# A pre-LN linear-attention block with an FFN on one core: the written order of 542 operations drawn anew, with the last five tiles' outputs finished in another sequence and the attention state copied on ScalarE

## The chip, the cores and the metric

The kernel runs on one core of a Trainium2 chip. The metric is device microseconds of that core, the median of three runs. The engines are named as in the profile: PE is TensorE's matmul, PEld its weight load, DVE is VectorE, ACT is ScalarE, POOL is GpSimd, and SP is the engine whose queue issues every DMA of this kernel.

## The reference

Inputs are bf16: x is 1 x 2048 x 512, wqkv 512 x 1536, wo 512 x 512, w1 512 x 1792, w2 1792 x 512. There are 32 heads of 16.

```python
phi = lambda t: jnp.where(t > 0, t + 1, jnp.exp(t)) + 1e-6
...
pq, pk = phi(q), phi(k)
kv = jnp.einsum("bhsd,bhse->bhde", pk, v)
z = jnp.einsum("bhsd->bhd", pk)
num = jnp.einsum("bhqd,bhde->bhqe", pq, kv)
den = jnp.einsum("bhqd,bhd->bhq", pq, z)[..., None] + 1e-6
o = num / den
...
x = A_x
h = x + _A_ref(_layernorm(x, axis=-1), A_wqkv, A_wo)
h2 = h + _B_ref(_layernorm(h, axis=-1), B_w1, B_w2)
return h2
```

`_A_ref` projects q, k and v, applies the attention above and the output projection wo; `_B_ref` is relu(x w1) w2.

## The kernel before, in words

The 2048 rows are 16 tiles t of 128 rows, in four chunks c of four tiles. Everything stays in SBUF, and PSUM is one tile `bk` of eight banks of 128 x 512 fp32. The body defines one small function `op_*` for each step. The string `ORDER` at the top lists 542 words, and the loop in lines 548 to 550 calls the functions in that order. A word is a name and its numbers: `K.5.3` is the key projection of tile 5 into bank 3, `f.13.4.7.7` is tile 13's second FFN product into bank 4, blocks 7 to 13. The order of the words on each engine is the order of that engine's queue; the framework adds the semaphore waits. No planner runs. What is moved in the string is moved on every engine that the word uses, SP's queue of DMA issues among them.

The steps, with the words that matter below:

- Layer norm of x: `lx` loads tiles; `S` and `A` are the statistics (DVE), `R` the two ACT steps of 1/sqrt, `N` the normalised tile (DVE). It is transposed either by PE (`T`) with a copy on ACT (`E`), for tiles 0 to 4, or by a DMA (`X`), for the others. `warm` is a run of matmuls on zeros into the bank that it names.
- Keys: `K` (four matmuls of 512 columns), then `F`, `U` on ACT and `M`, `D` on DVE for phi. `lk`, `lq`, `lv`, `lo`, `l1`, `l2` load rows of the weights. `G` accumulates phi(k)^T x-normalised in banks 4 to 7 over all tiles.
- Attention state: `gA` (ACT) or `gD` (DVE) copies two banks of that sum to `gT`; `kv`, `kx`, `m` make from it, wv and wo one 512 x 512 matrix per head block. `za`, `zf`, `z` sum the keys.
- Queries: `Q`, with `qF`, `qU`, `qM`, `qD` for phi. `dn`, `dnl`, `dnx` form 1/den, `dt` transposes it by DMA, `dm` scales the queries.
- `h` is the attention output of a tile (four matmuls), `hD` (DVE) adds x. `s`, `a`, `r`, `n` are the second layer norm; `x` transposes tile t by DMA to the chunk's `lnT`, `t` and `e` do it by PE and ACT for tile 2.
- FFN: `p.c.f.b` makes one block of 128 hidden columns for a whole chunk, so the first `p` of a chunk needs all four tiles' transposes. `pA` (ACT) or `pD` (DVE) is relu over two blocks. `f` is the product with w2: 14 matmuls for a tile, written as halves of seven; tile 15 is written as three column pieces of 128, 256 and 128.
- Output: `fo` (DVE) scales, adds h and writes to one of four buffers of `gT`; `fd` stores it (SP).

Of the kernel before, what the change touches and what calls it, by code (L numbers as in the profile page):

```python
# [23 lines left out]
lq.2.2 S.10 G.3 G.2 X.8 U.6.2 F.6.2 N.13 D.4.2 M.6.2 A.10 X.9 K.8.2 X.12 D.6.2 S.15 S.11 K.9.3 F.8.2 A.15 A.11
A.14 R.10.2 G.5 K.12.0 X.13 R.14.2 M.8.2 N.11 G.4 G.6 X.11 G.7 N.10 W.8.2 K.13.1 masks N.14 N.15 za.2 X.10 G.8
K.11.3 K.10.2 F.12.2 za.4 U.12.2 Q.0.0.0 F.10.2 X.14 U.10.2 Q.0.1.1 M.12.2 za.6 qU.0.0.2 G.9 M.10.2 X.15 K.14.2
l2.7.3 D.12.2 D.10.2 qF.0.0.2 G.12 K.15.3 za.8 qM.0.0.2 Q.0.2.0 za.10 F.14.2 lv.0.2 Q.0.3.1 U.14.2 za.12 M.14.2
D.14.2 G.13 G.10 zf.12 l1.2.2 G.11 G.14 qF.0.2.2 qM.0.2.2 G.15 z.0.2.14 z.3.2.14 z.2.2.14 lo.0.2 l2.0.3 z.1.2.14
Q.1.0.3 qD.0.0.2 qW.0.2.2 zc zh gA.0.2 dn.0.0 lv.2.2 Q.1.1.4 gD.2.2 l2.10.4 lo.2.2 kv.3.6 dnl.0 dnx.0.0.2
qF.1.0.2 kv.2.6 kv.0.6 dnx.0.2.2 kv.1.6 kx Q.1.2.0 Q.1.3.1 m.1.6 rt.2.2 m.0.5 qM.1.0.2 qW.1.0.2 rv.2 qF.1.2.2  # L30
dt.0 qM.1.2.2 dt.3 mA.0.2 Q.2.3.7 Q.3.1.3 dt.1 qW.1.2.2 m.3.5 l1.0.2 dm.0.0.2 m.2.4 Q.3.0.2 l2.3.4 mA.2.2 dn.1.1
dm.0.2.2 Q.2.2.6 h.3.5 h.0.0 h.2.4 hD.3 dnl.1 s.3 dnx.1.0.2 dnx.1.2.2 h.1.1 rt.6.5 hD.0 Q.3.2.0 qF.2.2.2
qU.3.0.2 a.3 dt.5 s.0 qF.3.0.2 hD.1 qU.2.2.2 a.0 hD.2 dt.4 n.0 Q.3.3.1 n.3 re.6 qF.3.2.2 Q.2.0.3 dt.7 s.1
qU.3.2.2 Q.2.1.4 dm.1.0.2 dm.1.2.2 a.1 h.4.6 qF.2.0.2 qM.2.2.2 x.0 n.1 qU.2.0.2 s.2 a.2 x.3 n.2 h.6.7 x.1 h.7.0
hD.6 t.2.5 s.6 h.5.1 qM.2.0.2 e.2 qD.2.2.2 qD.2.0.2 p.0.10.2 p.0.5.7 hD.5 dn.2.5 p.0.2.4 hD.4 dnl.2 hD.7
qM.3.0.2 p.0.11.3 dnx.2.0.2 qM.3.2.2 s.4 qD.3.2.2 s.5 a.6 r.0.4 dt.8 p.0.4.6 p.0.13.1 pA.0.10.2 dnx.2.2.2
p.0.0.2 dt.9 dt.11 p.0.1.3 p.0.12.0 pD.0.4.2 qD.3.0.2 pD.0.0.2 p.0.3.5 dt.10 dm.2.0.2 dn.3.2 dm.2.2.2 a.4
pA.0.12.2 dnl.3 dnx.3.0.2 n.6 p.0.6.6 p.0.9.3 h.8.0 p.0.7.7 pA.0.2.2 dnx.3.2.2 h.10.4 hD.10 hD.8 dt.12 x.6 s.7
dt.15 pA.0.6.2 p.0.8.2 dt.14 h.9.6 hD.9 s.10 h.11.0 pA.0.8.2 hD.11 f.3.2.0.7 a.7 a.5 dt.13 dm.3.0.2 f.0.4.0.7
f.2.7.0.7 n.5 n.4 dm.3.2.2 h.12.3 h.15.1 a.10 f.3.2.7.7 hD.12 hD.15 fo.3 h.14.0 s.9 a.9 n.10 n.7 f.2.7.7.7  # L40
f.0.4.7.7 f.1.1.0.7 s.15 s.11 fo.2 s.8 h.13.2 n.9 a.15 s.12 f.1.1.7.7 a.8 hD.14 x.5 n.8 x.7 s.14 a.11 a.12 x.4
hD.13 fd.3 p.1.10.0 s.13 p.1.3.6 a.13 fo.1 p.1.9.7 fo.0 n.15 p.1.7.2 p.1.6.1 n.12 fd.0 x.10 pA.1.6.2 p.1.12.3
n.13 a.14 p.1.2.5 p.1.13.4 pD.1.2.2 pA.1.12.2 fd.1 p.1.11.1 pA.1.10.2 x.8 n.11 x.11 p.1.5.5 r.12.4 p.1.4.4 n.14
# [5 lines left out]
f.8.5.7.7 p.3.11.2 p.3.1.7 fo.10 fo.8 p.3.12.3 pD.3.0.2 fo.11 fd.11 p.3.13.4 pA.3.12.2 pA.3.10.2 f.14.6.0.7
f.9.0.0.7 p.3.8.2 f.9.0.7.7 p.3.9.3 pA.3.8.2 fo.9 fd.8 f.12.5.0.7 f.12.5.7.7 f.14.6.7.7 fd.10 f.13.4.0.7 fd.9  # L50
# [530 lines left out]
```

## Time and profile before

| what | value |
|---|---|
| median of three runs | 171.25 us (171.04, 172.23, 171.25) |
| the profiled execution's own time | 170.93 us |
| its span, first to last instruction | 169.2 us |
| mean granted TensorE clock | 0.998 |
| PE, DVE, ACT busy | 162.3, 102.4, 65.5 us |
| moved by DMA | 15.36 MB, of it 7.86 read from and 2.10 written to HBM |

The lines of the timeline give start and length in us, then engine, line of the kernel, operation, tiles (output <- inputs) and how many in a row; a bracket names how long the engine stood idle before and what ended that. SPq is SP's DMA queue; its length is that of the issue, and the time to landing stands in a row of its own. Of the 875 matmuls, 859 have a record in this trace.

### The profile page before, as it was taken

The page shows a single profiled execution, that of the slowest core. Times are in us where ns is not written, and L with a number is a line of the kernel's source. Part 1 is how long each engine was busy: PE and PEld are TensorE (multiplying, and loading weights), DVE is VectorE, ACT ScalarE, POOL GpSimd, SP SyncE. Part 2 cuts the span into 40 slices and gives each one's busy share as a digit, 9 for nine tenths or more (in the row PEclk, how much of TensorE's full clock was granted, in tenths as well). Part 3 has the DMA queues.
Part 4 walks back from the last instruction along what each step waited for, and adds up shares of the span by engine and source line. Part 5 has one row for each costly group of instructions (what it writes and reads, how often), then busy time and mean ns, then how long its engine had stood idle before and what let it go on. Part 6 is the DMA issues. An engine that isn't in the chain of part 4 may idle for free.

```text
span 169.2 us, 2285 instructions
## 1 busy us (share of the span) xinstructions
PE 162.3 (96%) x859; PEld 76.2 (45%) x875; DVE 102.4 (61%) x202; ACT 65.5 (39%) x95; POOL 4.8 (3%) x21
## 2 busy tenths in 40 slices
...
DMA packets 29947, 15.36 MB, mean 91 GB/s; under 512 B 22640, under 2 KB 28784, under 8 KB 29936
## 3 DMA queue, kind: packets, MB, share of 16 engines
...
q8 instruction: 7, 0.11, 0.3%
q14 instruction: 4, 0.03, 0.1%
HBM read 7.86 MB, written 2.10 MB: 59 GB/s over the span
## 4 chain that ended last, share of the span: by engine, by line
PE 89%; DVE 5%; DMA 3%; issue 1%; ACT 0%
PE bk L510 29%; PE bk L530 28%; PE bk L307 8%; PE bk L494 8%; PE bk L351 8%; PE bk L299 6%; DVE st L226 3%; DMA x_nat<-in_A_x_dram 2%; DMA lnT<-h_nat 2%; PE bk L448 1%; DVE h_nat L251 1%; PE bk L392 1%; PE bk L404 1%; PE bk L270 0%; DVE mv L227 0%
## 5 line engine op out<-in xcount | busy, mean ns | idle before, releaser
L510 PE MATMUL bk<-lnT,w_sb 128*128 128x512 bf16 x219 | 51.0, 379 | 0.4
L530 PE MATMUL bk<-w_sb,at 128*128 128x512 bf16 (+2 forms) x249 | 50.9, 355 | 0.1
L516 ACT ACTIVATE at<-bk 128x1024 bf16<-128x1024 f32 x16 | 16.1, 1020 | 70.1 <-PE bk L510 70.1
L530 PEld LDWEIGHTS <-at 128*128 128x128 bf16 x252 | 23.6, 98 | 25.2
L538 DVE SCALAR_TENSOR_TENSOR gT<-bk,rstd,h_nat 128x512 bf16<-128x512 f32 (+2 forms) x18 | 12.0, 686 | 36.0 <-PE bk L530 28.8
L510 PEld LDWEIGHTS <-w_sb 128*128 128x128 bf16 x224 | 21.8, 98 | 26.0 <-issue 0.2
L521 DVE TENSOR_SCALAR at<-bk 128x1024 bf16<-128x1024 f32 x12 | 14.5, 1219 | 13.5 <-PE bk L510 13.4
L317 ACT ACTIVATE eb<-bk 128x1024 bf16<-128x1024 f32 (+1 forms) x17 | 16.6, 975 | 6.9 <-PE bk L299 6.7
L299 PE MATMUL bk<-wk_sb,lnT 128*128 128x512 bf16 x63 | 16.0, 380 | 1.4 <-DMA wk_sb<-in_A_wqkv_dram 1.0
L307 PE MATMUL bk<-lnT,wq_sb 128*128 128x512 bf16 x61 | 14.9, 379 | 0.2
L494 PE MATMUL bk<-m_sb,pqs 128*128 128x512 bf16 x61 | 15.0, 379 | 0.1
L351 PE MATMUL bk<-at,h_nat 128*128 128x512 bf16 x55 | 13.2, 379 | 0.1
L500 DVE TENSOR_TENSOR h_nat<-bk,x_nat 128x512 bf16<-128x512 f32 x16 | 10.6, 678 | 4.0 <-PE bk L510 2.2
L320 ACT ACTIVATE rb<-bk 128x1024 bf16<-128x1024 f32 (+1 forms) x13 | 12.4, 964 | 0.0
L226 DVE BATCH_NORM_STATS2 st<-x_nat 128x6 f32<-128x512 bf16 x16 | 10.5, 679 | 2.3 <-DMA x_nat<-in_A_x_dram 2.3
L228 DVE BATCH_NORM_STATS2 st<-h_nat 128x6 f32<-128x512 bf16 x16 | 10.9, 686 | 0.1
L299 PEld LDWEIGHTS <-lnT 128*128 128x128 bf16 x64 | 5.7, 98 | 9.3 <-ACT lnT L280 2.6
L351 PEld LDWEIGHTS <-h_nat 128*128 128x128 bf16 x64 | 6.3, 98 | 7.5
L494 PEld LDWEIGHTS <-pqs 128*128 128x128 bf16 x64 | 6.1, 98 | 7.5 <-DVE pqs L484 1.0
L307 PEld LDWEIGHTS <-wq_sb 128*128 128x128 bf16 x64 | 5.9, 97 | 6.3
L461 ACT ACTIVATE wk_sb<-ld 128x1024 bf16<-128x1024 f32 x8 | 8.3, 1050 | 0.1
L484 DVE TENSOR_TENSOR pqs<-pqT,rd 128x1024 bf16<-128x1024 bf16 x8 | 5.2, 685 | 3.8 <-DMA rd<-wk_sb 2.3
...
## 6 DMA issues: line engine op xcount, KB each, us to landing
...
w_sb<-in_B_w_dram SPq DMA_DIRECT2D x2, 384.0 KB, 5.7
...
```

Source lines behind the costliest of these rows:

```text
L226: op_S = lambda t: nc.vector.bn_stats(out=st[:, t, :], in_=x_nat[:, t, :])
L299: nc.tensor.matmul(bk[:, b, :], lhsT=lnT[c][:, kd, j * P : (j + 1) * P], rhs=wk_sb[:, kd, :], start=(kd == 0), stop=(kd == KD - 1),)
L307: nc.tensor.matmul(bk[:, b, :], lhsT=wq_sb[:, kd, j * P : (j + 1) * P], rhs=lnT[c][:, kd, :], start=(kd == 0), stop=(kd == KD - 1),)
L317: nc.scalar.activation(out=buf(eb, kind, i, n), in_=bank(at_bank[kind, i], n), func=ACT.Exp)
L320: nc.scalar.activation(out=buf(rb, kind, i, n), in_=bank(at_bank[kind, i], n), func=ACT.Relu)
L351: nc.tensor.matmul(bk[:, KD + kd, :], lhsT=ln_nat[:, t, kd * P : (kd + 1) * P], rhs=pk(t)[:, 0, :], start=(t == 0), stop=(t == NT - 1),)
L494: nc.tensor.matmul(bk[:, b, :], lhsT=pqs[:, (c * KD + jb) % NQ, j * P : (j + 1) * P], rhs=m_sb[:, jb, :], start=(jb == 0), stop=(jb == KD ...
L510: nc.tensor.matmul(bk[:, b, cols], lhsT=w1_sb[:, kd, f * P : (f + 1) * P], rhs=lnT[c][:, kd, cols], start=(kd == 0), stop=(kd == KD - 1),)
L516: nc.scalar.activation(out=acts[c % 2][:, f : f + n, :], in_=bank(at_bank["p", c, f], n), func=ACT.Relu)
L521: nc.vector.tensor_scalar(out=acts[c % 2][:, f : f + n, :], in0=bank(at_bank["p", c, f], n), scalar1=0.0, scalar2=None, op0=ALU.max,)
L530: nc.tensor.matmul(bk[:, b, 0 : w * P], lhsT=acts[c % 2][:, f, j * P : (j + 1) * P], rhs=w2_sb[:, f, k * P : (k + w) * P], start=(f == 0), ...
L538: nc.vector.scalar_tensor_tensor(out=o_t[:, t % NO, cols], in0=bk[:, at_bank["f", t, k], 0 : w * P], scalar=rstd2[:, t : t + 1], in1=h_nat ...
```

## The change

Only the string `ORDER` is changed. It has 542 words before and after. Other than the sequence, these words differ: some banks; `gD.2.2` becomes `gA.2.2`, so both copies of the attention state are on ACT; of the relus, five go from ACT to DVE (`pA.0.2`, `pA.3.4`, `pA.3.6`, `pA.3.8`, `pA.3.10` become `pD`) and two from DVE to ACT (`pD.2.0` and `pD.3.0` become `pA`); 11 warm-up matmuls stay 11, but before they are all ahead of `T.0`, and now nine are ahead of it and two behind it. The start and the end of the string:

```diff
-const lx.0.1 lx.1.1 lx.2.2 S.0 warm.1.1 table A.0 S.1 warm.1.1 R.0.1 N.0 A.1 lk.0.2 S.3 warm.9.1 S.2 T.0.5 R.1.1
+const lx.0.1 lx.1.1 S.0 lx.2.2 table A.0 S.1 R.0.1 A.1 R.1.1 lk.0.2 N.0 S.3 warm.9.6 S.2 T.0.1 warm.1.6 lk.2.2
...
-f.13.4.7.7 f.15.0.0.14.3.1 fo.13 fo.15.3.1 fo.14 fd.15.3.1 f.15.2.0.14.0.2 fo.12 fd.13 fd.14 fo.15.0.2
-f.15.4.0.14.2.1 fo.15.2.1 fd.12 fd.15.0.2 fd.15.2.1
+f.14.6.0.7 p.3.8.2 f.9.1.0.7 f.9.1.7.7 pD.3.8.2 fo.9 f.14.6.7.7 fd.8 f.15.0.0.14.3.1 fd.11 fd.9 f.13.7.7.7
+fo.15.3.1 fo.14 f.12.5.7.7 fo.13 fd.15.3.1 f.15.2.0.14.0.2 fo.12 fd.14 fd.13 fo.15.0.2 fd.12 f.15.6.0.14.2.1
+fo.15.2.1 fd.15.0.2 fd.15.2.1
```

First place, ACT's queue in the head, from the key projection of tile 0 on. L280 is the copy behind a PE transpose (`E`), L317 and L320 are `F` and `U`, L232 and L233 the two steps of `R`:

```order
 L317 ACTIVATE eb<-bk 128x512
 L320 ACTIVATE rb<-bk 128x512
-L280 ACTIVATE lnT_81<-bk 128x4x128 x2
+L280 ACTIVATE lnT_81<-bk 128x4x128
+L317 ACTIVATE eb<-bk 128x512
+L280 ACTIVATE lnT_81<-bk 128x4x128
 L232 ACTIVATE rstd<-mv,eps_73 128x2
 L233 ACTIVATE rstd<-rstd 128x2
 L320 ACTIVATE rb<-bk 128x512
-L317 ACTIVATE eb<-bk 128x512
```

Tile 1's `F` moves from behind the root of tiles 4 and 5 to a place ahead of it, between `E.3` and `E.2`, which change places with each other. On DVE, `A.1` moves from behind `N.0` to a place ahead of it:

```order
 L226 BN_STATS st<-x_nat 128x6
+L227 BN_AGGR mv<-st 128x2
 L251 TENSOR_SCALAR h_nat<-x_nat,mv,rstd 128x512
-L227 BN_AGGR mv<-st 128x2
 L226 BN_STATS st<-x_nat 128x6 x2
```

The first row is `S.1`, the third `N.0`, the last `S.3` and `S.2`; only the aggregate is moved.

Second place, SP's queue in the middle. L480 is `dt`, L292 is `x` (lnT_82 is chunk 1, lnT_83 chunk 2), L204 loads three blocks of w2 (`l2.0.3`), L545 is a store of the output:

```order
-L480 DMA_TRANSPOSE rd<-wk_sb 128x4x128 x5
+L480 DMA_TRANSPOSE rd<-wk_sb 128x4x128 x4
+L204 DMA w_sb<-in_B_w_dram 128x3x512
+L480 DMA_TRANSPOSE rd<-wk_sb 128x4x128 x2
 L292 DMA_TRANSPOSE lnT_82<-hn 128x4x128
-L480 DMA_TRANSPOSE rd<-wk_sb 128x4x128 x3
-L292 DMA_TRANSPOSE lnT_82<-hn 128x4x128 x3
-L545 DMA out_dram<-gT 128x512 x2
+L480 DMA_TRANSPOSE rd<-wk_sb 128x4x128 x2
+L292 DMA_TRANSPOSE lnT_82<-hn 128x4x128
+L545 DMA out_dram<-gT 128x512
+L292 DMA_TRANSPOSE lnT_82<-hn 128x4x128 x2
```

The load of w2's first three blocks, which stood among the other weight loads near 31 us, now stands behind the transposes of chunk 2's denominators, and the store of tile 3 (`fd.3`) now stands between `x.5` and the last two transposes of chunk 1, `x.7` and `x.4`. The words that lead from there to chunk 1's first `p`, after:

```text
h.15.4 hD.12 hD.15 fo.3 a.10 s.11 a.11 f.0.7.7.7 h.14.4 s.15 f.2.2.7.7 h.13.6 f.1.1.7.7 fo.2 a.15 n.10 a.9 hD.14 n.9
s.12 hD.13 a.8 x.5 fd.3 x.7 fo.0 x.4 fo.1 x.9 p.1.10.0
```

In the same way `lq.0.2` leaves the first loads, where `lv.2.2` now stands, for a place between `X.12` and `X.13`.

Third place, the last outputs on DVE (L538 is `fo`), with the semaphores that each waits for. Before:

```order
L538 SCALAR_TENSOR_TENSOR gT<-bk,rstd_103,h_nat 128x512 [waits DVE_49,DMAHW0_49,PE_49,Activation_49]
L538 SCALAR_TENSOR_TENSOR gT<-bk,rstd_103,h_nat 128x128 [waits DMAHW5_49,PE_49]
L538 SCALAR_TENSOR_TENSOR gT<-bk,rstd_103,h_nat 128x512 [waits DMAHW7_49]
L538 SCALAR_TENSOR_TENSOR gT<-bk,rstd_103,h_nat 128x512 [waits DMAHW6_49]
L538 SCALAR_TENSOR_TENSOR gT<-bk,rstd_103,h_nat 128x256 [waits PE_49,Activation_49]
L538 SCALAR_TENSOR_TENSOR gT<-bk,rstd_103,h_nat 128x128 [waits PE_49]
```

These are tile 13, the first piece of tile 15, tiles 14 and 12, and the two last pieces of tile 15: tiles 14 and 12 wait for no matmul of their own. After:

```order
L538 SCALAR_TENSOR_TENSOR gT<-bk,rstd_103,h_nat 128x128 [waits DMAHW7_49,DVE_49,PE_49]
L538 SCALAR_TENSOR_TENSOR gT<-bk,rstd_103,h_nat 128x512 [waits DMAHW5_49]
L538 SCALAR_TENSOR_TENSOR gT<-bk,rstd_103,h_nat 128x512 [waits DMAHW0_49,DVE_49,PE_49]
L538 SCALAR_TENSOR_TENSOR gT<-bk,rstd_103,h_nat 128x512 [waits DMAHW6_49,PE_49]
L538 SCALAR_TENSOR_TENSOR gT<-bk,rstd_103,h_nat 128x256 [waits PE_49]
L538 SCALAR_TENSOR_TENSOR gT<-bk,rstd_103,h_nat 128x128 [waits PE_49]
```

Now the first piece of tile 15 and tile 14 come first, and tiles 13 and 12 each wait for their own last matmuls. In SP's queue the stores follow as 15's first piece, 14, 13, 12 and 15's last two.

More of the change, by code (lines that the diff above doesn't have):

```diff
@@ L24 @@
[L24 to L43, printed above, removed]
@@ L49 @@
[L49 to L52 removed]
+const lx.0.1 lx.1.1 S.0 lx.2.2 table A.0 S.1 R.0.1 A.1 R.1.1 lk.0.2 N.0 S.3 warm.9.6 S.2 T.0.1 warm.1.6 lk.2.2
+A.3 lx.4.2 A.2 lx.6.2 warm.1.6 E.0 N.1 K.0.1.0.2 lx.8.4 T.1.4 R.2.2 K.0.1.2.2 N.3 N.2 S.5 E.1 S.4 T.3.5 T.2.7
@@ new lines @@
+G.8 K.11.3 K.10.2 F.12.2 za.4 za.6 M.12.2 U.12.2 F.10.2 Q.0.1.1 Q.0.0.0 G.9 D.12.2 M.10.2 U.10.2 qF.0.0.2 za.8
+D.10.2 G.12 X.15 X.14 lv.0.2 za.10 l2.7.3 l1.2.2 qU.0.0.2 lo.0.2 K.14.2 K.15.3 Q.0.3.1 G.10 qM.0.0.2 lo.2.2
+Q.0.2.0 G.13 za.12 qD.0.0.2 F.14.2 U.14.2 qF.0.2.2 M.14.2 D.14.2 zf.12 G.14 G.11 qM.0.2.2 z.2.2.14 G.15 z.1.2.14
+z.0.2.14 z.3.2.14 Q.1.0.3 qW.0.2.2 zc zh gA.0.2 dn.0.0 Q.1.1.4 gA.2.2 kv.1.5 dnl.0 dnx.0.0.2 qF.1.0.2 kv.2.5
+kv.0.5 kv.3.5 kx dnx.0.2.2 l2.10.4 Q.1.3.1 Q.1.2.0 m.1.6 rt.2.2 m.0.5 qM.1.0.2 qW.1.0.2 rv.2 Q.2.3.7 qF.1.2.2
@@ new lines @@
+dt.0 qM.1.2.2 mA.0.2 Q.3.1.3 dt.3 m.3.5 dt.1 m.2.4 qW.1.2.2 l2.3.4 l1.0.2 dm.0.0.2 Q.3.0.2 mA.2.2 dn.1.0
+dm.0.2.2 Q.2.2.6 h.3.5 dnl.1 hD.3 h.0.0 h.2.4 dnx.1.0.2 dnx.1.2.2 qF.3.0.2 s.3 qF.2.2.2 h.1.1 qU.2.2.2 rt.6.5
+hD.0 Q.3.2.0 a.3 dt.5 dt.4 s.0 qU.3.0.2 hD.1 a.0 hD.2 dt.7 n.0 Q.3.3.1 s.1 n.3 Q.2.1.4 re.6 qU.3.2.2 qF.3.2.2
+Q.2.0.3 dm.1.0.2 dm.1.2.2 qF.2.0.2 a.1 x.0 n.1 qU.2.0.2 s.2 qM.2.2.2 a.2 x.3 h.6.2 qM.2.0.2 n.2 x.1 h.7.0 h.4.6
+hD.6 t.2.5 hD.7 h.5.1 e.2 qD.2.2.2 qD.2.0.2 p.0.10.2 p.0.5.7 dn.2.5 hD.4 p.0.4.6 dnl.2 p.0.11.3 hD.5 s.4
```

28 lines of the change are left out of this document (19 added, 9 removed).

## The prediction

> **What bounds the kernel now.** I read the page first, then busy time in stretches, then the chain of waits in order of time, then the store queue at the end.
>
> ```profile
> span 169.2 us, 2285 instructions
> PE 162.3 (96%) x859; PEld 76.2 (45%) x875; DVE 102.4 (61%) x202; ACT 65.5 (39%) x95; POOL 4.8 (3%) x21
> ...
> 5.46:19.68 14.22, 12.64 (x69) 5.22 (x69) 13.88 (x41) 12.76 (x27) 0.67 (x3) 1.00 0.72 210
> 19.68:93.38 73.70, 73.25 (x426) 35.25 (x434) 61.87 (x121) 38.77 (x49) 0.00 (x0) 1.00 0.47 115
> 93.38:165.75 72.37, 72.00 (x357) 34.27 (x362) 24.02 (x33) 12.21 (x17) 0.00 (x0) 1.00 0.14 36
> 165.75:169.20 3.45, 0.22 (x4) 0.05 (x1) 0.38 (x2) 0.00 (x0) 0.00 (x0) 0.91 0.46 140
> ```
>
> In the stretches the first number is the length, then busy us of PE, PEld, DVE, ACT and POOL. From 19.68 to 165.75 PE is busy 145.25 of 146.07 us. The 0.82 us that are missing are 16 matmuls without a record (859 against 875 weight loads), each a false gap of 0.05 in the chain. So nothing waits there: with the same matmuls, a new order can gain nothing in those 146 us and can only open holes. Room exists in two places. In the head, 5.46 to 19.68, PE idles 1.58 us, but there DVE is busy 13.88 of 14.22: the head is DVE's stream. The other is the end.
>
> ```profile
> 108.06 6.04 PE bk L530 x28
> ...
> 154.50 0.75 DVE L538 SCALAR_TENSOR_TENSOR gT<-bk,rstd,h_nat 128x512 bf16<-128x512 f32 x1 [5.24 <-PE bk L530]
> 155.28 0.33 SPq L545 DMA_DIRECT2D out_dram<-gT  x1
> ...
> 165.79 1.39 SPq L545 DMA_DIRECT2D out_dram<-gT  x3
> 166.01 0.35 DVE L538 SCALAR_TENSOR_TENSOR gT<-bk,rstd,h_nat 128x128 bf16<-128x128 f32 x1 [0.23 <-PE bk L530]
> 166.78 0.40 SPq L545 DMA_DIRECT2D out_dram<-gT  x1
> ```
>
> The first row gives the price of a 512-wide matmul in a full stream: 6.04/28 = 0.216 us. The rest is the end: the last DVE operation is done at 166.36, and a store can be issued 0.03 us after DVE is done (155.25, 155.28), so at 166.39. It is issued at 166.78, because three stores stand in SP's queue, (1.39-0.40)/2 = 0.495 us apart. The end loses 0.39 us to that queue.
>
> **The change, part by part.**
>
> *The end.* Before, DVE took tiles 13, 14 and 12 one right behind the other once tile 13 was complete, and their stores piled up. Now tiles 14, 13 and 12 are completed in this order, 13 and 12 by seven matmuls each, 7 x 0.216 = 1.51 us apart. Count back from the last DVE operation, which starts at 166.01. The last group (14 matmuls of 128 columns) takes 14 x 0.054 = 0.76, the one before (14 of 256) 1.51. So tile 12 reaches DVE near 163.7, is done 0.75 later, near 164.5, and is stored then, not at 165.79. The 256 columns reach DVE at 165.25 and take between the 0.35 of 128 columns and the 0.75 of 512, say 0.5: their store goes out near 165.8 and frees SP near 166.3, before 166.39. The last store then waits for DVE alone: **-0.39**. Bounds: -0.39, and 0 if one store more still stands ahead. The output has four buffers, and the stores that must land before tiles 13, 12 and 15 may be written are issued some 3 us earlier; cover enough.
>
> *The head.*
>
> ```profile
> 4.31 0.66 DVE L226 BATCH_NORM_STATS2 st<-x_nat 128x6 f32<-128x512 bf16 x1
> 4.99 0.41 DVE L251 TENSOR_SCALAR h_nat<-x_nat,mv,rstd 128x512 bf16<-128x512 bf16 x1
> 6.84 0.59 PE L299 MATMUL bk<-wk_sb,lnT 128*128 128x512 bf16 x2 [0.98 <-DMA wk_sb<-in_A_wqkv_dram]
> 9.14 1.11 ACT L280 ACTIVATE lnT<-bk 128x512 bf16<-128x512 bf16 x2
> 10.43 0.29 ACT L232 ACTIVATE rstd<-mv,eps 128x2 f32<-128x2 f32 x1 [0.18 <-DVE mv L227]
> 11.29 0.40 DVE L251 TENSOR_SCALAR h_nat<-x_nat,mv,rstd 128x512 bf16<-128x512 bf16 x1
> 11.72 3.90 SPq L291 DMA_TRANSPOSE lnT<-h_nat  x3
> 19.67 0.33 PEld L299 LDWEIGHTS <-lnT 128*128 128x128 bf16 x3 [0.49 <-DMA lnT<-h_nat]
> ```
>
> The last hole of PE, at 19.67, waits for X.8, which stands behind X.5 to X.7 in SP's queue, and that queue starts at 11.72, when N.5 (11.29 to 11.69) is done. So N.5 sets the head. A.1 now goes ahead of N.0: it must wait for S.1's end at 4.97, and N.0 slips from 4.99 to about 5.1. That delay ends in PE's wait for wk_sb at 6.84, and the same work stands ahead of S.3, so DVE's stream moves by some 0.03. On ACT, E.3, F.1 and E.2 now come ahead of the square root for N.5. E.2 and E.3 took 1.11 us together from 9.14; a third of that kind, 0.5 more, puts the root's first step near 10.8 instead of 10.43 and the end of its second near 11.3 (each 0.2 to 0.3), so N.5 starts near 11.34. Sum of the head: **+0.05**. Bounds: -0.1 (DVE's stream holds no more) and +0.3 (if ACT's three slip further). lv.2.2 in the old place of lq.0.2 is a load of the same size. lq.0.2 is now issued behind X.12, takes 0.6 us of SP ahead of X.13, and is wanted only at the first Q, near 29.
>
> *The warm-up.*
>
> ```profile
> 1.25 4.27 PE L215 MATMUL bk<-m_sb 128*128 128x512 bf16 x11 [1.25 <-DVE ones L177]
> ...
> L215 PE MATMUL bk<-m_sb x11: 379/634/634, 1.2 to 5.1; 128*128 128x512 bf16 x11
> ```
>
> Eleven either way, but two of them now follow T.0, in the wait for wk_sb: two at 0.216 from about 5.8 are over by 6.84. Take 8 slow ones and 3 fast ones: (4.27 - 0.38 - 2 x 0.216)/8 = 0.43 us for a slow one, so the slow ones (634 ns long) end near 4.7 in both orders, and the clock comes up within the ninth: **0**. The Trainium skill, "TensorE: Matmul & The Clock Gate", Part 1: The HAM clock gate, speaks against opening a hole here: the array runs at half rate until about 3.4 us of sustained work have passed in a window that runs freely. This trace agrees on the length (1.25 to about 4.7), and by the page the sum stays 0 here unless the window's phase falls on the new hole.
>
> *The attention state, and relus that change engine.*
>
> ```profile
> L384 ACT ACTIVATE gT<-bk 128x1024 bf16<-128x1024 f32 x1 | 1.0, 1023 | 2.8 <-PE bk L351 2.8
> ...
> L387 DVE CAST gT<-bk 128x1024 bf16<-128x1024 f32 x1 | 1.2, 1217 | 0.0
> ...
> L516 ACT ACTIVATE at<-bk 128x1024 bf16<-128x1024 f32 x16 | 16.1, 1020 | 70.1 <-PE bk L510 70.1
> L521 DVE TENSOR_SCALAR at<-bk 128x1024 bf16<-128x1024 f32 x12 | 14.5, 1219 | 13.5 <-PE bk L510 13.4
> ```
>
> The second copy moves from DVE (1.22) to ACT (1.02), behind the first. PE did not wait for either, since query projections stood ahead of kv: **0** in each direction. Of the relus, net three go from ACT to DVE, 0.2 us longer each, 0.6 in all. The tightest is the last, tiles 8 and 9 of the last chunk: 14 matmuls (3.0 us) now stand between p.3.8 and the first reader, against some 1.5 us of DVE and latency: **0**. If that cover went, at most 0.6.
>
> *Two transfers moved behind other waits.* These decide the sign.
>
> ```profile
> 19.08 2.53 SPq L291 DMA_TRANSPOSE lnT<-h_nat  x2
> ...
> 25.73 1.03 PE L299 MATMUL bk<-wk_sb,lnT 128*128 128x512 bf16 x4
> 68.95 1.26 SPq L480 DMA_TRANSPOSE rd<-wk_sb  x1
> 77.68 4.70 PE L530 MATMUL bk<-w_sb,at 128*128 128x512 bf16 x21
> w_sb<-in_B_w_dram SPq DMA_DIRECT2D x2, 384.0 KB, 5.7
> ```
>
> l2.0.3, 384 KB, was loaded near 31 and is now issued behind the four transposes that end at 70.21. The first f wants it at 77.68. Two loads of that size took a median of 5.7 us: landed near 76, **0**. It would have to take over 7.4.
>
> ```profile
> 87.75 1.19 SPq L292 DMA_TRANSPOSE lnT<-hn  x1
> 89.37 1.35 SPq L292 DMA_TRANSPOSE lnT<-hn  x1
> 90.78 0.56 SPq L545 DMA_DIRECT2D out_dram<-gT  x1
> 93.22 2.75 PE L510 MATMUL bk<-lnT,w_sb 128*128 128x512 bf16 x12
> 94.19 1.38 DVE L538 SCALAR_TENSOR_TENSOR gT<-bk,rstd,h_nat 128x512 bf16<-128x512 f32 x2
> 95.59 0.36 SPq L545 DMA_DIRECT2D out_dram<-gT  x1
> 96.04 1.19 SPq L292 DMA_TRANSPOSE lnT<-hn  x1
> ...
> DMA to landing us min/median/max: 2.4/2.4/4.1
> ...
> DMA to landing us min/median/max: 3.5/3.5/3.5
> ```
>
> The last two rows are for all 15 transposes of L292, and for the one at 89.37 alone, x.4. It landed at 92.87, and chunk 1's first matmul starts at 93.22: 0.35 us to spare. Now the store fd.3 stands ahead of x.7 and x.4, and SP takes them in turn. fd.3 waits for fo.3, which on DVE follows hD.15, which waits for h.15. Between h.15's end and p.1.10.0 stand 29 matmuls (7 + 4 + 7 + 4 + 7), so h.15's last starts 30 x 0.216 = 6.47 before 93.22, at 86.75, and is done 0.38 later (2.75 - 11 x 0.216). hD.15 starts near 87.2, fo.3 0.64 behind it (the pair at 94.19), and ends at 88.6. fd.3 is issued then; the transpose behind a store follows after 0.45 (95.59, 96.04) to 0.62, and x.4 follows x.7 after 1.25 to 1.62 (87.75, 89.37). So x.4 starts between 90.3 and 90.9, instead of 89.37. At the median of 2.4 it lands at 92.7 to 93.3, at its own 3.5 at 93.8 to 94.4. PE waits **0** at the one and 0.6 to 1.2 at the other. I take 0, because the median of 15 transposes is 2.4 and those that followed other stores are in it; both ends stay in the range.
>
> *Sum.* 169.2 + 0.05 - 0.39 = 168.86 of span. What lies around it is 170.93 - 169.2 = 1.73 in the profiled execution, which gives 170.59, or -0.34. The median of the three runs shown is 171.25, 0.32 above the profiled execution, so I put the difference on the median: **170.9 us**.
>
> **The rivals.**
>
> *x.4 comes too late (slower than before).* The place is p.1.10.0 near 93.2, and the price is what x.4 lands after 93.2: 0.6 to 1.2 with its old 3.5 us, and up to 1.8 with the longest, 4.1. From 0.34 us on it eats the gain. At its middle, 0.9, the time is 171.8. For it: two of 15 transposes were late, and x.4 is one of them. Against it: the other 13 took about 2.4.
>
> *The end gains nothing.* If a store still stands in SP's queue, the change does not do what it says there: 171.25 + 0.05 = 171.3. Against it: the gaps worked out above all exceed the 0.495 of a store.
>
> *Another load or transpose is late.* X.13, the second of the pair at 19.08, started near 20.4 and now starts near 21.0, behind lq.0.2; K.13 wants it at 25.73, 4.7 us later, where the slowest transpose took 4.1; l2.0.3 has 7.4. With 0.5 us of stall at either: 171.4.
>
> *The clock comes up later.* If the new hole near 5 us costs another slow stretch like the 3.4 us of the trace, K.0's four matmuls and the transposes around them run slow: 4 x 0.255 = 1.0, part of it hidden in DVE's stream, so 0.7 and 171.6. That is the case which the section of the Trainium skill named above leaves open.
>
> **How the numbers follow.** Forecast 170.9: 0.55. x.4 late, 171.8: 0.25. No gain at the end, 171.3: 0.08. Another late transfer, 171.4: 0.07. The clock, 171.6: 0.05. The range runs from 170.5 (the head at -0.1, and some 0.3 that runs differ) to 172.0 (x.4 with 1.1 of wait); it leaves out the longest wait at x.4 and little else. Over 1% is 1.7 us, about what a measurement here can tell from no change. Faster than that would need 1.7 us from a head and an end that hold 1.58 and 0.39 together: 0.01. Slower than that, over 172.96, needs x.4 beyond its longest row, or two of the rivals at once: 0.05. Within 1%: 0.94.
>
> **What would show it.** The last store issued within 0.1 us of the last DVE operation's end confirms the end. The hole at X.8 near 19.7 dates the head. A PE wait for lnT near 93 is x.4, one for w_sb near 77.7 is l2.0.3. PE idle over 0.3 us anywhere else between 19.7 and 165.8 would prove me wrong, as would slow matmuls after 5.5.

## The result, and the profile after

The changed kernel takes 172.45 us (median of 14 runs, 171.70 to 173.07) against 171.45 for the kernel before (14 runs, 170.93 to 172.23). The ratio is 1.0056, with a 95% interval of 1.0038 to 1.0074: 1.0 us slower, where 170.9 was forecast and the range ended at 172.0. The profiled execution took 172.27 us with a span of 170.6, against 170.93 and 169.2; unrounded the spans are 170.56 and 169.21, so 1.34 us of span are what the two traces have to explain. In some executions of two kernels below, `e2` and `e3`, the clock fell behind a long hole of PE; their medians are over all runs, their ratios without those.

The page and busy time in stretches, of the changed kernel; the stretches are cut where PE starts on X.8's tile, where it starts p.1.10.0, and at its last matmul:

```profile
span 170.6 us, 2295 instructions
PE 163.3 (96%) x859; PEld 76.2 (45%) x875; DVE 105.6 (62%) x204; ACT 63.7 (37%) x93; POOL 4.8 (3%) x21
```

```profile
5.46:20.45 14.99, 13.38 (x68) 5.07 (x67) 14.66 (x43) 12.56 (x25) 0.64 (x3) 1.00 0.77 203
20.45:95.02 74.57, 73.30 (x424) 35.12 (x433) 60.45 (x113) 38.52 (x48) 0.00 (x0) 1.00 0.47 113
95.02:167.55 72.53, 72.16 (x356) 34.38 (x364) 27.92 (x40) 10.38 (x15) 0.00 (x0) 1.00 0.16 41
167.55:170.60 3.05, 0.23 (x5) 0.05 (x1) 0.35 (x1) 0.00 (x0) 0.00 (x0) 0.95 0.13 33
```

The row of the last stretch runs to 170.60, but the last instruction ends at 170.56. From the start of the last matmul to the end of the span it is 3.00 us instead of 3.46, 0.46 less, where 0.39 was forecast. The first stretch ends at 20.45 instead of 19.68, 0.77 later. The second lacks 1.27 us of PE where its counterpart lacked 0.45. The groups of PE instructions say what it waited for:

```profile
L510 PE MATMUL bk<-lnT,w_sb 128*128 128x512 bf16 x220 | 50.6, 379 | 1.1 <-DMA lnT<-hn 0.8
L299 PE MATMUL bk<-wk_sb,lnT 128*128 128x512 bf16 x63 | 15.9, 380 | 1.3 <-DMA lnT<-h_nat 0.7 <-ACT lnT L280 0.5
```

Both are transposes by DMA that landed late: x.4 ahead of p.1.10.0, and X.8 in the head. I count a hole as the time from one matmul's start to the next, less 0.216. By that count p.1.10.0 has 0.99 (93.82 to 95.02, none before) and X.8 0.85 (before: 0.16); 0.07 more stand at h.7.0 near 58.9.

*x.4.* SP's queue, then DVE, then PE, of the changed kernel:

```profile
82.51 1.19 SPq L292 DMA_TRANSPOSE lnT<-hn  x1
89.36 0.36 SPq L545 DMA_DIRECT2D out_dram<-gT  x1
89.76 5.46 SPq L292 DMA_TRANSPOSE lnT<-hn  x3
...
84.79 0.67 DVE L500 TENSOR_TENSOR h_nat<-bk,x_nat 128x512 bf16<-128x512 f32 x1
87.98 0.69 DVE L500 TENSOR_TENSOR h_nat<-bk,x_nat 128x512 bf16<-128x512 f32 x1 [2.52 <-PE bk L494]
88.59 0.74 DVE L538 SCALAR_TENSOR_TENSOR gT<-bk,rstd,h_nat 128x512 bf16<-128x512 f32 x1
...
95.03 3.18 PE L510 MATMUL bk<-lnT,w_sb 128*128 128x512 bf16 x14 [0.82 <-DMA lnT<-hn]
```

The view of L292 for the one instance at 91.40, which is x.4:

```profile
L292 SPq DMA_TRANSPOSE lnT<-hn x1: 1421/1421/1421, 91.4 to 91.4; - x1
...
  PE bk L510: 0.8, 1
...
DMA to landing us min/median/max: 3.4/3.4/3.4
```

SP issues x.5 at 82.51 and then nothing for nearly 6 us: fd.3 waits for fo.3, which stands on DVE behind hD.15's wait of 2.52 us for PE. x.7 and x.4 go only behind it. x.4 lands at 94.78, 0.75 after PE was up, that is ready for p.1.10.0 (94.03).

*X.8.* From the chain of waits in order of time, of the changed kernel:

```profile
16.42 3.98 DMA lnT<-h_nat
20.45 1.90 PE bk L299 x8
```

X.8 was issued at 16.42, 0.09 later than before, and took 3.98 us to land instead of 3.3. The view of X.8 before:

```profile
DMA to landing us min/median/max: 3.3/3.3/3.3
```

*The end,* of the changed kernel:

```profile
165.50 0.75 DVE L538 SCALAR_TENSOR_TENSOR gT<-bk,rstd,h_nat 128x512 bf16<-128x512 f32 x1 [0.76 <-PE bk L530]
167.03 0.48 DVE L538 SCALAR_TENSOR_TENSOR gT<-bk,rstd,h_nat 128x256 bf16<-128x256 f32 x1 [0.78 <-PE bk L530]
167.81 0.35 DVE L538 SCALAR_TENSOR_TENSOR gT<-bk,rstd,h_nat 128x128 bf16<-128x128 f32 x1 [0.30 <-PE bk L530]
...
168.19 0.33 SPq L545 DMA_DIRECT2D out_dram<-gT  x1
```

The last DVE operation ends at 168.16 and its store goes out 0.03 later. Before, 0.42 lay between.

So the span's difference is 0.77 (head) + 0.07 + 0.99 (x.4) - 0.46 (end) = 1.37, for a measured 1.34. Whether these are the order's doing or one execution's was for the runs to tell.

### The profile page after: what moved, and what is told of

It reads as the page before. It is cut to its first block, busy times and chain, and to the rows that moved or that the text cites. A ratio compares the mean times of both kernels' runs of the same rounds, so it can differ in the third digit from the quotient of the medians.

```text
span 170.6 us, 2295 instructions
## 1 busy us (share of the span) xinstructions
PE 163.3 (96%) x859; PEld 76.2 (45%) x875; DVE 105.6 (62%) x204; ACT 63.7 (37%) x93; POOL 4.8 (3%) x21
## 4 chain that ended last, share of the span: by engine, by line
PE 82%; DVE 9%; DMA 5%; issue 1%; SPq 0%; ACT 0%; DVEq 0%
PE bk L530 27%; PE bk L510 26%; PE bk L307 8%; PE bk L494 7%; PE bk L351 6%; PE bk L299 4%; DVE st L226 4%; DMA lnT<-h_nat 2%; DMA x_nat<-in_A_x_dram 2%; DVE h_nat L251 1%; DVE gT L538 1%; PE bk L448 1%; DVE st L228 1%; DVE h_nat L500 1%; DVE hn L258 1%
## 5 line engine op out<-in xcount | busy, mean ns | idle before, releaser
L516 ACT ACTIVATE at<-bk 128x1024 bf16<-128x1024 f32 x13 | 13.3, 1020 | 68.3 <-PE bk L510 68.3
L521 DVE TENSOR_SCALAR at<-bk 128x1024 bf16<-128x1024 f32 x15 | 18.3, 1221 | 31.2 <-PE bk L510 31.2
L538 DVE SCALAR_TENSOR_TENSOR gT<-bk,rstd,h_nat 128x512 bf16<-128x512 f32 (+2 forms) x18 | 12.1, 687 | 15.3 <-PE bk L530 15.3
L317 ACT ACTIVATE eb<-bk 128x1024 bf16<-128x1024 f32 (+1 forms) x17 | 16.3, 976 | 8.3 <-PE bk L299 7.5
L320 ACT ACTIVATE rb<-bk 128x1024 bf16<-128x1024 f32 (+1 forms) x13 | 12.4, 965 | 0.0
```

The lines of the kernel that those rows point to most:

```text
L317: nc.scalar.activation(out=buf(eb, kind, i, n), in_=bank(at_bank[kind, i], n), func=ACT.Exp)
L516: nc.scalar.activation(out=acts[c % 2][:, f : f + n, :], in_=bank(at_bank["p", c, f], n), func=ACT.Relu)
L521: nc.vector.tensor_scalar(out=acts[c % 2][:, f : f + n, :], in0=bank(at_bank["p", c, f], n), scalar1=0.0, scalar2=None, op0=ALU.max,)
L538: nc.vector.scalar_tensor_tensor(out=o_t[:, t % NO, cols], in0=bk[:, at_bank["f", t, k], 0 : w * P], scalar=rstd2[:, t : t + 1], in1=h_nat ...
```

## The experiments

My theory was that fd.3's wait in SP's queue costs about 1 us at x.4, that the end is worth what was forecast, and that lq.2.2, the load directly ahead of X.8, makes X.8 late. The rivals were that the changed head itself is slow, and that any store ahead of a transpose costs. Each kernel changes only the string of words. Their strings fill two lines less, so their line numbers are two lower (L290 for L292). Ratios are to the kernel before on the same chip, with 95% intervals; an interval of 0.0018 either way is 0.3 us.

### The store behind x.4, the load behind X.9, and the new end alone

```diff
-x.5 fd.3 x.7 fo.0 x.4 fo.1
+x.5 x.7 fo.0 x.4 fd.3 fo.1
```

> The changed kernel with one word moved: the store fd.3 behind x.4 instead of ahead of x.7 and x.4. Theory (SP's queue: x.7 and x.4 stood behind a store that waited for DVE until 89.3): x.7 and x.4 are issued near 84 to 85 as soon as their inputs are there, chunk 1's last transpose lands before 90, PE's wait of 0.99 us at the first p of chunk 1 (94.0 to 95.0) is gone, and the time falls by 0.8 to 1.0 us against the changed kernel. Rival (x.4 is late because a code fetch hits it, wherever it stands): the last transpose still takes 3.4 us, but from an earlier start; then the wait is gone too only if the start moves, and if the start does not move the wait stays at 0.5 to 1.0.

Measured 170.86 us (170.38 to 171.57), ratio 0.9973 (0.9957 to 0.9988), where the changed kernel had 1.0056. SP's queue and PE of this kernel:

```profile
82.54 4.63 SPq L290 DMA_TRANSPOSE lnT<-hn  x3
89.38 0.36 SPq L543 DMA_DIRECT2D out_dram<-gT  x1
...
94.06 3.18 PE L508 MATMUL bk<-lnT,w_sb 128*128 128x512 bf16 x14
```

x.7 and x.4 go 5.5 to 6 us earlier, and PE starts p.1.10.0 without a hole. The store goes out when it did before the move.

```diff
-K.7.1 lq.2.2 S.10 G.3 G.2 X.8 ... A.10 X.9
+K.7.1 S.10 G.3 G.2 X.8 ... A.10 X.9 lq.2.2
```

> The changed kernel with one word moved: the 256 KB load lq.2.2 behind X.9 instead of ahead of X.8. Theory (X.8 lands late because it stands behind that load's data): X.8 is issued near 15.8 instead of 16.4 and lands in 2.4 to 2.6 us, near 18.3, so PE's hole of 0.85 us ahead of K.8 near 19.6 to 20.4 vanishes and the time falls by 0.6 to 0.9. Rival (the hole comes from the 8 KB code fetch at 18.2, not from the load): X.8 has landed before the fetch, or lands late by the same 0.7 because a fetch hits it; a fall under 0.3 would speak for that.

Measured 173.38 us over all 12 runs (171.37 to 175.78), ratio 1.0073 (1.0038 to 1.0109): no better than the changed kernel's 1.0056. In the profiled execution, which took 175.61, X.8 did land 2.8 us after its issue and PE did not wait for it, but the load now stood directly ahead of X.12, which took 4.9. PE and the stretch behind, of this execution:

```profile
24.32 1.37 PE L297 MATMUL bk<-wk_sb,lnT 128*128 128x512 bf16 x4 [2.25 <-DMA lnT<-h_nat]
```

```profile
22.00:24.30 2.30, 0.07 (x1) 0.00 (x0) 2.07 (x7) 1.15 (x5) 0.00 (x0) 1.00 1.11 167
24.30:28.40 4.10, 4.08 (x12) 1.53 (x13) 4.07 (x6) 0.00 (x0) 0.00 (x0) 0.58 0.47 91
```

A hole of 2.4 us, and behind it 4.1 us in which the mean granted clock was 0.58. In this execution the harm had moved from one transpose to the next. Five of the 12 runs took 171.4 to 172.2 us; no trace shows those, and a hole of this size hardly fits into them.

> Both moves in the changed kernel. If the two waits add up and nothing else takes their place: 1.4 to 1.9 us below the changed kernel, that is 0.4 to 0.8 us below the kernel before, with no hole of PE over 0.3 us after 14.5 us. If the waits overlap or another wait takes their place: no better than the better of the two single moves.

With both moves: 172.81 us (170.79 to 175.32), ratio 1.0009 (0.9975 to 1.0042). In the profiled execution (174.46) there is no hole at p.1.10.0 and the same one at X.12 (2.6 us). The one move did not touch the other's hole.

The fourth has every word of the order before up to tile 12's first half, and the new end behind it:

```diff
-fd.8 f.12.5.0.7 ... (the old end)
+fd.8 f.12.5.0.7 f.13.4.0.7 fd.10 f.14.6.7.7 fd.9 f.15.0.0.14.3.1 f.13.4.7.7 fo.15.3.1 fo.14 f.12.5.7.7 fo.13
+fd.15.3.1 f.15.2.0.14.0.2 fo.12 fd.14 fd.13 fo.15.0.2 fd.12 f.15.6.0.14.2.1 fo.15.2.1 fd.15.0.2 fd.15.2.1
```

> The kernel before with the new finish alone: the last words (tiles 13, 14, 12 and 15 and their stores) in the changed kernel's sequence, everything ahead of them as before. Theory (the end lost 0.39 us to SP's queue): the last store is issued within 0.05 us of the last DVE operation's end, 0.39 us earlier against PE's last matmul, and the time is 0.3 to 0.4 us below the kernel before. Rival (the end is set by how long the last stores take to land together, not by their issue): the issue moves but the end does not, under 0.15 us.

Measured 170.71 us (170.25 to 170.91), ratio 0.9953 (0.9935 to 0.9970). The end alone is a gain, -0.8 us by the ratio, with -0.5 as its near bound, more than the 0.3 to 0.4 expected. In this trace the last matmul starts 3.00 us ahead of the end of the span, again 0.46 less than before, and the last store goes out 0.03 us behind DVE:

```profile
166.29 0.35 DVE L536 SCALAR_TENSOR_TENSOR gT<-bk,rstd,h_nat 128x128 bf16<-128x128 f32 x1 [0.23 <-PE bk L528]
...
166.67 0.33 SPq L543 DMA_DIRECT2D out_dram<-gT  x1
```

### Is it the store's place, or its wait?

The same move of fd.3 in the order before with the new end. In the order before, fo.3 ends at 86.4, ahead of x.7's own data at 87.7:

```diff
-x.5 n.8 x.7 s.14 a.11 a.12 x.4 hD.13 fd.3 p.1.10.0
+x.5 fd.3 n.8 x.7 s.14 a.11 a.12 x.4 hD.13 p.1.10.0
```

> The order before with the new tail, and fd.3 moved ahead of x.7 and x.4, the place it has in the changed kernel. Theory (what costs is the wait of a store for a late fo.3, not a store ahead of a transpose): here fo.3 ends at 86.67 and x.7 is issued at 88.02, when n.7 is done, so fd.3 goes out in an idle time of SP's queue, x.7 stays at 88.0, and the time stays that of the order before with the new tail, 0.995 of the kernel before, within 0.2 us of 170.7. Rival (each store ahead of x.7 and x.4 makes them late): x.4 lands 0.5 us later or more, PE idles 0.2 to 1.5 us ahead of p.1.10.0, and the time is 171.0 to 172.2. Beside it: SP's 80th instruction was x.4 in four traces, where it landed 3.4 to 3.5 us after its issue, and is x.7 here. If the 8 KB code fetch that follows SP's 79th instruction delays whatever stands 80th, x.7 takes 3.4 us and x.4 2.5; if x.4 is late for another reason, x.4 keeps its 3.5.

Measured 170.58 us (170.01 to 171.22), ratio 0.9965 (0.9947 to 0.9982), the same as with the new end alone. SP's queue of this kernel:

```profile
81.72 1.19 SPq L290 DMA_TRANSPOSE lnT<-hn  x1
86.51 0.36 SPq L543 DMA_DIRECT2D out_dram<-gT  x1
87.83 2.51 SPq L290 DMA_TRANSPOSE lnT<-hn  x2
```

The store goes out in idle time and x.7 stays where it was. The place is free where the store is ready. The expectation's side question had an answer too: x.7, during which the fetch of SP's code now fell, took 2.4 us, and x.4 2.4 too.

In the changed kernel, with only x.4 behind the store:

```diff
-x.5 fd.3 x.7 fo.0 x.4
+x.5 x.7 fd.3 fo.0 x.4
```

> The changed kernel with fd.3 between x.7 and x.4: x.7 goes near 83.8 and only x.4 waits behind the store for fo.3. Theory (the cost is what x.4 lands after PE is up with p.1.10.0, near 94.0): fd.3 is issued at 89.4, x.4 at 89.8 to 90.2, and lands at 92.3 to 93.7 with 2.5 to 3.5 us; PE does not wait and the time is that with fd.3 behind x.4, 170.9 within 0.3 us. Rival (any transpose behind the waiting store costs the same): PE idles about 1 us ahead of p.1.10.0 and the time is 172.0 to 172.5.

Measured 171.00 us (170.59 to 171.35), ratio 0.9981 (0.9966 to 0.9997). x.4 went at 89.80 instead of 91.40, landed in 2.4 us at 92.2, and PE started p.1.10.0 at 94.06 without waiting.

And with the store where the change put it, but fo.3 ahead of hD.15 on DVE, in the time in which DVE waited for PE:

```diff
-hD.12 hD.15 fo.3 a.10
+hD.12 fo.3 hD.15 a.10
```

> The changed kernel with fo.3 ahead of hD.15 on DVE, where DVE stood idle from 85.46 to 87.98; the store fd.3 keeps its place ahead of x.7 and x.4. Theory (the cost is the wait of the store for fo.3, which stood behind the wait for h.15): fo.3 runs near 85.6 to 86.4, fd.3 is issued near 86.4, x.7 near 86.8 and x.4 near 88.1, x.4 lands at 90.5 to 91.5, the hole of 1 us goes, and the time is that with fd.3 behind x.4 or between x.7 and x.4, 170.8 to 171.2. Rival (a store ahead of x.7 and x.4 costs by itself): a hole stays, 171.6 to 172.4.

Measured 171.17 us (170.58 to 172.01), ratio 0.9997 (0.9975 to 1.0018). DVE, then SP's queue, then PE of this kernel:

```profile
85.51 0.75 DVE L536 SCALAR_TENSOR_TENSOR gT<-bk,rstd,h_nat 128x512 bf16<-128x512 f32 x1
87.89 0.69 DVE L498 TENSOR_TENSOR h_nat<-bk,x_nat 128x512 bf16<-128x512 f32 x1 [1.62 <-PE bk L492]
...
86.29 0.36 SPq L543 DMA_DIRECT2D out_dram<-gT  x1
86.69 8.44 SPq L290 DMA_TRANSPOSE lnT<-hn  x3
...
93.94 4.26 PE L508 MATMUL bk<-lnT,w_sb 128*128 128x512 bf16 x19
```

fd.3 goes 3.1 us earlier and the hole is gone. Three ways of taking the wait away (0.9973, 0.9981, 0.9997, mean 0.9984) against the changed kernel twice (1.0056, and 1.0036 below, mean 1.0046): the wait costs 0.0062, 1.1 us, about the hole of the trace. That is its price together with x.4's late landing, which all three ways took away too.

### The load away from X.8

In the order before with the new end, and in the changed kernel with the store behind x.4, lq.2.2 moved behind X.13, where the next transpose, X.11, is issued 1.8 us or more later:

```diff
-lq.2.2 S.10 G.3 G.2 X.8 ... X.13
+S.10 G.3 G.2 X.8 ... X.13 lq.2.2
```

> The order before with the new tail, and the load lq.2.2 moved from ahead of X.8 to behind X.13. Theory (a transpose issued within 0.7 us behind a 256 KB load lands 3.3 to 4.9 us after its issue instead of 2.5): X.8 lands near 18.7, before PE's keys of tile 8 are up at 19.4, and PE's hole of 0.33 us there goes; X.11, issued near 24.0, may land 1 us later, near 27.5, still before K.11 near 28. The time is 170.3 to 170.5, against 170.7 with lq.2.2 ahead of X.8. Rival (the load only moves the harm): a hole of 0.5 us or more for X.11 or X.10 near 28, or for the first Q near 29.8, and 170.9 to 171.7.

Measured 170.20 us (169.94 to 170.58), ratio 0.9941 (0.9922 to 0.9961).

> The changed kernel with fd.3 behind x.4 and lq.2.2 behind X.13, where lq.0.2 stands ahead of X.13. Theory: X.8 lands 2.5 to 2.8 us after its issue and its hole of 1.04 us in the profile with lq.2.2 ahead of it goes; the time is 170.2 to 170.6, against 170.9. X.12 keeps its 2.5 us since no load stands directly ahead of it (with lq.2.2 there it took 4.9). Rival: two loads close together hold X.11 back beyond K.11 near 28, a hole of 0.5 to 2 us, 171 to 173.

Measured 170.29 us (169.97 to 171.23), ratio 0.9941 (0.9923 to 0.9959). X.8 lands 2.6 and 2.8 us after its issue, PE starts on it without a hole (at 19.29 and 19.54), X.11 lands in 2.5, and no new hole stands. PE on X.8's tile, in the one and in the other:

```profile
19.29 1.89 PE L297 MATMUL bk<-wk_sb,lnT 128*128 128x512 bf16 x8
...
19.54 1.89 PE L297 MATMUL bk<-wk_sb,lnT 128*128 128x512 bf16 x8
```

These two are the fastest of all kernels. That they are equal says more: with both transposes in time, the changed order in the head and the middle (banks, relus, the copy on ACT, the warm-up) costs nothing against the old one, within the 0.3 us of an interval.

X.8 over all traces:

| X.8 | us from issue to landing | hole of PE |
|---|---|---|
| lq.2.2 ahead, head as before (3 traces) | 3.2 to 3.5 | 0.04 to 0.33, mean 0.18 |
| lq.2.2 ahead, changed head (8 traces) | 3.4 to 4.2 | 0.26 to 1.04, mean 0.71 |
| lq.2.2 elsewhere (5 traces) | 2.6 to 2.8 | none |

By the ratios the changed head costs 0.0025 with the load ahead of X.8 (mean 0.9984 against 0.9953 and 0.9965), 0.4 us, about the 0.5 of the traces.

Is it the load, or a fetch of code? In all 16 traces 8 KB of code are fetched within X.8's time as well. Where that fetch began 0.64 to 0.75 us behind X.8's issue in the changed head, X.8 took 3.8 us with the load ahead (one trace) and 2.8 without (four traces). So the load holds it, and not the fetch alone.

### Why x.4 took 3.4 us

With the usual 2.4 us, x.4 would have landed near 93.85 (an estimate from its issue at 91.41), before PE was up at 94.03, store or no store. In the traces up to here a packet of kind "instruction", 8 KB of code, began 1.06 to 1.16 us behind the end of SP's 79th instruction, and a second 0.2 to 0.4 us behind the start of hD.14 on DVE. The first experiment split one load, so that the first fetch falls ahead of x.4; the changed kernel ran again beside it.

```diff
-kx dnx.0.2.2 l2.10.4 Q.1.3.1
+kx dnx.0.2.2 l2.10.2 l2.12.2 Q.1.3.1
```

> The changed kernel once more, for a second trace of it on the chip of the next kernel. Theory (x.4 lands 3.4 to 3.5 us after its issue whenever an 8 KB code fetch falls into its first 2.05 us, which it does in this order): PE's hole ahead of p.1.10.0 is there again, 0.9 to 1.1 us, while the hole at X.8, a stall of a transpose behind a load, may be anything from 0.1 to 1.1. Median 172.2 to 172.6, ratio 1.004 to 1.008. Rival (the late landing was chance): no hole or another one at p.1.10.0, and a median nearer to 171.5.

172.05 us (171.65 to 172.89), ratio 1.0036 (1.0014 to 1.0057); the hole at p.1.10.0 is there again, 0.98, and X.8's is 0.89.

> The changed kernel with one load of w2, l2.10.4, written as two of half the size, some 60 us ahead of x.4, so that x.4 stands one place later in SP's queue; fd.3 still stands ahead of x.7 and x.4. In eight traces an 8 KB code fetch began 1.06 to 1.15 us behind the end of the same instruction of SP, the 79th. Theory (what makes x.4 late is the code fetch of SP): the fetch now follows the end of fd.3, falls into x.7 or earlier, the 0.37 us more between x.7 and x.4 go too, x.4 is issued near 91.0, lands near 93.5 with 2.5 us, before PE is up with p.1.10.0 near 94.0, the hole goes, and the time is 170.9 to 171.5 with the store still where it was. Rival 1 (x.4 is late because it waits behind a store): x.4 keeps 3.4 us, lands near 94.4 to 94.8, hole 0.6 to 1.0, time 172.0 to 172.5. Rival 2 (x.7 takes the delay on): x.7 lands 1 us late near 93.2, still before 94.0, and the time is as in the theory.

Measured 171.88 us (171.30 to 172.97), ratio 1.0028 (1.0009 to 1.0048). The first fetch did move, to 90.21, 0.7 us ahead of x.4's issue, and x.7 beside it took 2.45 us. x.4 still took 3.4, and PE waited:

```profile
94.45 3.83 PE L508 MATMUL bk<-lnT,w_sb 128*128 128x512 bf16 x16 [0.86 <-DMA lnT<-hn]
```

So SP's fetch is not the cause. Next I moved DVE's count, by two relus on ACT.

```diff
-pD.0.4.2 ... pD.0.0.2
+pA.0.4.2 ... pA.0.0.2
```

> The changed kernel with two early relus of chunk 0, pD.0.4 and pD.0.0, on ACT, near 70 us, so that DVE has two instructions less ahead of 93 us; fd.3 stays ahead of x.7 and x.4. In eleven of twelve traces a second 8 KB code fetch began while DVE was in its 191st instruction, the addition hD.14; in the seven where it began 1.84 to 2.03 us after x.4's issue x.4 took 3.37 to 3.50 us, in the five where it did not 2.41 to 3.06. Theory (this fetch of DVE's code holds x.4's last landing): the 191st instruction is now two operations later, near 93.9, the fetch begins near 94.1, x.4 is issued at 91.4 as before and lands at 93.8 to 93.9, PE finds lnT ready at 94.0, the hole of 0.98 to 1.02 us ahead of p.1.10.0 goes, and the time is 171.0 to 171.5. Rival (x.4 is late for what stands ahead of it in SP's queue): x.4 takes 3.4 us whatever DVE's count is, the hole stays 0.9 to 1.0 and the time 171.9 to 172.5.

Measured 172.38 us (171.95 to 173.00), ratio 1.0071 (1.0044 to 1.0098). The theory failed: the second fetch did not follow DVE's count. hD.14 was now DVE's 189th instruction, and the fetch still began 0.26 us behind its start. x.4 took 3.36 us and the hole was 0.98.

> The kernel with the two early relus on ACT, and lq.2.2 behind X.13 beside it: the two holes that the changed kernel's trace shows, 0.69 more at X.8 and 0.99 at p.1.10.0, are both taken away without moving a store or touching the end. Theory: the gains add up, 170.2 to 170.6, what the kernel with fd.3 behind x.4 and lq.2.2 behind X.13 took (170.29). Rival (the store ahead of x.7 and x.4 costs by itself): 171.0 to 171.7.

Measured 171.62 us (171.21 to 172.56), ratio 1.0030 (1.0011 to 1.0048). X.8's hole went, x.4's stayed (1.26, with 3.66 us to landing). Beside it this trace has a head that came 0.35 later, where S.5 waited for the load of x's tiles 4 and 5, and a hole of 0.32 near 72, where PE waited for a step of ACT that stood behind one of the added relus; so the gains did not add up to 170.3.

Last, x.4 later with the fetch in place:

```diff
-hD.15 fo.3 a.10 s.11 a.11
+hD.15 a.10 s.11 fo.3 a.11
```

> The changed kernel with fo.3 behind a.10 and s.11 on DVE instead of ahead of them, so that fo.3, fd.3, x.7 and x.4 all come 0.83 us later (0.17 + 0.66); hD.14 and the matmuls are not moved. Theory (the second 8 KB code fetch, 0.2 to 0.4 us behind the start of hD.14, holds x.4's last landing until 1.35 to 1.8 us after the fetch began): x.4 is issued near 92.2, the fetch begins near 93.3, x.4 lands near 94.8, 2.6 us after its issue, the hole ahead of p.1.10.0 stays 0.9 to 1.1 and the time 172.0 to 172.5. Rival (x.4 takes 3.4 us in this order whatever the fetch does): x.4 lands at 95.6, the hole is 1.7 to 1.9 and the time 172.8 to 173.3.

Measured 172.32 us (171.97 to 173.28), ratio 1.0068 (1.0040 to 1.0096).

```profile
94.72 3.61 PE L508 MATMUL bk<-lnT,w_sb 128*128 128x512 bf16 x16 [1.23 <-DMA lnT<-hn]
```

x.4 came 0.65 later against hD.14 and took 3.1 us; the hole grew by 0.4, to 1.39. That is between the two expectations, 0 and 0.7 to 0.9 more, and decides for neither. What stands over all traces is a coincidence: in ten traces the second fetch began 1.1 to 2.0 us after x.4's issue, and x.4 took 3.1 to 3.7; in five where this fetch began at another time it took 2.4 to 2.5. (In the one that is left, 3.1, a 16 KB packet of the same kind began 0.2 us ahead of x.4's issue.)

The packets within these traces say more than the coincidence. A transpose is 512 packets of 256 bytes and behind them 32 of 4 bytes. In the changed kernel x.4's 256-byte packets are done at 93.36, and 30 of the 4-byte packets have begun by 93.63. The last two begin at 93.91, when the second code packet (93.43 to 93.91) ends, and x.4 lands 0.86 later. Six traces have this packet at x.4's end and no store beside it: in all six the last two begin within 0.02 us of its end, and x.4 lands 0.8 to 1.05 behind them. In the five traces with 2.4 to 2.5 us the last two begin with the others, and x.4 lands 0.33 to 0.37 behind them. So by the packets' times x.4's data had moved before PE was up; what came late was the end of the transfer, behind the fetch of code. No run takes the fetch away by itself, and why the landing then follows half a microsecond slower is not known.

## Why the prediction was wrong

*The step that failed* is the landing of x.4: "I take 0, because the median of 15 transposes is 2.4 and those that followed other stores are in it; both ends stay in the range." The steps ahead of it held. h.15, hD.15, fo.3, fd.3, x.7 and x.4 followed one another as worked out: x.4 was issued 2.6 us before PE was up (91.40 against 94.03), where 2.3 to 2.9 was forecast. Then it took 3.4 us, its own duration of before, and the hole was 0.99, inside the "0.6 to 1.2 at the other". The rival "x.4 comes too late" was what happened, at the place and for the price given, with a chance of 0.25. The choice between two ends was made by the median of a group where the row of the instance itself stood in the fence: x.4 took 3.5 before, 3.4 now, and 3.4 to 3.7 in five of the six other traces in which it waited behind the store for a late fo.3 (3.1 in the sixth). A landing that is late in one trace at one place is to be taken as that place's price, not as chance, until a second trace says otherwise. What made it hold here could not be read from that row: the second fetch follows the start of hD.14, which comes 1.7 us behind x.4's issue before and 1.6 after. Where x.4 was issued 2.1 us or more ahead of hD.14 (five traces with 2.4 to 2.5, one with 3.1), the price was not paid.

*The head, +0.05, was mis-sized.* N.5's part was right: K.5.3 starts at 14.42 instead of 14.33, +0.09. But the working took X.8's landing as fixed, and it is not. It went from 3.3 to 4.0 in the two profiles, and the hole was 0.71 on the mean of eight traces against 0.18. Near 0.4 to 0.5 us is what the changed head costs, over the bound of +0.3 that I gave. The load directly ahead of X.8 is shown to be the cause of the late landing, since without it X.8 takes 2.6 to 2.8 in both orders. In all eleven traces with the load ahead, X.8 lands 0.5 to 0.7 us behind the load itself, and the load takes 3.4 us on the mean in the head as before and 4.0 in the changed one. Why the same load takes longer in the changed head is not settled. The stall lies inside the transfers, as the share of DMA shows (packets are counted where they begin, so a share over 1 means packets that take long). Before, and after:

```profile
18.50:19.00 0.50, 0.50 (x4) 0.23 (x3) 0.50 (x3) 0.50 (x2) 0.00 (x0) 1.00 0.96 110
19.00:19.75 0.75, 0.75 (x5) 0.17 (x3) 0.75 (x3) 0.75 (x2) 0.00 (x0) 1.00 0.92 173
```

```profile
18.50:19.00 0.50, 0.50 (x4) 0.23 (x3) 0.50 (x2) 0.50 (x1) 0.00 (x0) 1.00 2.84 122
19.00:19.75 0.75, 0.75 (x4) 0.16 (x2) 0.75 (x3) 0.75 (x2) 0.00 (x0) 1.00 0.58 23
```

The same half microsecond holds packets of 2.84 shares instead of 0.96, and in the next the core moves 23 GB/s instead of 173.

*The end, -0.39, was right in its mechanism and in the trace:* -0.46 in the changed kernel and with the end alone. Of this 0.39 is the store's issue, 0.03 us behind DVE instead of 0.42, and 0.07 comes after it. By the ratios it is worth more, 0.0041 on the mean of two kernels, 0.7 us. The 0.2 to 0.3 between them is the size of one interval, and the profiled execution of before was 0.5 us faster than the median of its 14 runs; no run tells these apart.

*Right at 0:* l2.0.3 landed 3.5 us after its issue, at 74.6, without a wait; lq.0.2 and X.13 landed at 24.7 and 25.3 without a hole; relus and the copy on ACT show no hole; two warm-ups behind T.0 cost nothing, though the clock did come up later: the ninth warm-up still runs its full 634 ns, and the two behind T.0 stand 0.43 apart, up to 6.4. So the rival of the clock, and its sign, slow matmuls after 5.5, did show, but without its price of 0.7: DVE still set the head. Nor was it the order's doing: in the twelve traces that record it, the clock comes up between 4.1 and 7.0 us, and at 7.0 in the kernel with the new end alone, whose head is that of before. K.0 started at 6.39 instead of 6.84, since its weights landed earlier.

*The sum by the ratios:* end -0.7, head +0.4, x.4 +1.1: +0.8, between the changed kernel's two measurements (0.6 and 1.0). The range ended at 172.0 because it added x.4's 1.1 to the forecast, but nothing for a head beyond its bound. Another 0.2 lies in the base: the kernel before has a median of 171.25 in three runs and 171.45 in 14.

One reading of the prediction was off without effect: it put the 0.82 us that PE lacks from 19.68 to 165.75 down to 16 matmuls without a record. By its own rows there are 783 matmuls and 796 weight loads there, so about 13 of the 16, which at 0.05 each make up 0.65 us.
